# Clustered attention and a gated block: four more heads multiply with their centroids in 12 matmuls of 32 columns, in a re-ordered list of steps

## The chip, the cores and the metric

The kernel runs on one core of a Trainium2 chip. The core has five engines that run side by side, each with a queue of its own that it works through in order: TensorE (PE, matmuls; weight loads are shown apart as PEld), VectorE (DVE), ScalarE (ACT), GpSimd (POOL) and SyncE (SP), which here only issues DMAs. The metric is the device time of one execution in microseconds (us), lower is better.

## The reference

Four batches, eight heads, 768 tokens, 64 features per head. Each query and each key is assigned to the centroid, of 16 of its head, with the largest cosine. A query attends only to keys of its own centroid. A dense gated block follows.

```python
q_assign = np.argmax(np.einsum('bhsd,hcd->bhsc', q_n, c_n), axis=-1)
k_assign = np.argmax(np.einsum('bhsd,hcd->bhsc', k_n, c_n), axis=-1)
mask = q_assign[:, :, :, None] == k_assign[:, :, None, :]
scores = np.where(mask, scale * np.matmul(q, k.transpose(0, 1, 3, 2)), -1000000000.0)
scores = scores - np.max(scores, axis=-1, keepdims=True)
attn = np.exp(scores)
attn = attn / (np.sum(attn, axis=-1, keepdims=True) + 1e-09)
x = np.matmul(attn, v)                 # then (tokens, 512)
h = x @ w_in                           # 512 x 2048
out = (h * (1.0 / (1.0 + np.exp(-h)))) @ w_out   # 2048 x 512
```

Inputs and output are float32.

## The kernel before, in words

**Order.** The whole kernel after a short preamble is one list of some 1,550 words (`plan`, from line 722). A word is a step: `qk51` is step `qk` of number 51; after a point comes an engine (A = ACT, D = DVE, P = POOL) or the PSUM bank that it opens (0 to 3). The function `step` issues the word's instructions to their engines in the order of the list. So each engine meets its own instructions in list order, waits for what they read, and everything behind a waiting instruction on the same engine waits too. PE has four single banks and two double ones (`st`); a word that opens a bank waits until the last user of that bank has been read out.

**A head.** A head (b, h) has the number 8b + h. Its steps, in order:
- `r` loads queries and keys (two DMAs on SP); `vl` loads values (SP or POOL).
- `hi` and `lo` split the raw tile into two float16 parts (`lo` on DVE, L112; `hi` on ACT L103, POOL L105 or DVE L107).
- `ht` transposes it by a DMA on SP (L121) into the tile `ab`, for heads 8 to 31; heads 0 to 7 use PE and `ev`.
- `L` or `l` multiplies the 12 blocks of 128 tokens with the centroids on PE (L159). `L` does two matmuls of 16 columns for each block, which add up the two parts of the centroids in PSUM. `l` does one matmul of 32 columns, and `ls` (DVE, L168) then adds the two halves.
- `mx` (L183) and `ge` (L192), both on DVE, make the one-hot matrix of assignments.
- Heads 8 to 15: `cm` turns it on PE (L221), `ce` evicts it (ACT L232 or DVE L234) and sends it by a DMA on SP (L235) into spare rows of `ab`. Heads 16 to 31: `cs` scales on POOL (L199, L200), `cx` transposes by a DMA on SP (L208), `cv` moves it by a DMA on POOL (L212) into those rows. The rows make the mask part of the score matmul.
- `qk` (PE, L325, two matmuls of 384 columns, 192 of them) makes scores; `ex` (ACT, L330) the exponentials. Six `qk` belong to each head, three for each half of the queries. Heads 8 to 15 start at qk48, 51, 54 and so on; head 16 at qk96; head 21 at qk111; head 30 at qk162.
- `v` casts the values, `pv` (PE, L342) multiplies for two heads, `nm` (DVE, L352 and L354) normalizes, `pt` and `pe` or `xd` (a DMA on SP, L381) transpose the result.

**The dense block.** `e` (PE, L390, four matmuls) computes 128 of the 2048 hidden features for 384 tokens, `t` (ACT, L402) a tanh, `g` (DVE, L405) the gate. `w` loads weights by POOL; `wc` (DVE, L443) combines pieces of w_out once. For the second matrix one 128-token tile uses 16 plain matmuls in four words `b` (L417), with `bo` for its output, and pairs of tiles use Strassen's seven products `m` (L477), with sums `S` (DVE, L490), `z` (ACT, L499) and outputs `o` (L505, L508).

The two forms of the centroid product differ by the argument `w` of one function (line 149), and by where the list calls `ls`:

```python
        for n in ns or range(2 * m):
            i = min(n, job.n - 1)
            for x in range(0, 2 * HC, w):
                nc.tensor.matmul(
                    L[:, n % 2, :, n // 2], ab[:, i, :], stk[:, job.groups[i // 3][0], x : x + w],
                    start=(x == 0), stop=(x + w == 2 * HC),
                )
```

Of the kernel before, what the change touches and what calls it, by code (L numbers as in the profile page):

```python
# [29 lines left out]
def kernel(  # L30
# [573 lines left out]
    def step(op, n, eng, banks):  # L604
# [145 lines left out]
        ex74 qk76 m4 S14 xd9 xd8 ex75 qk77 z12 v14.A pv11.1 o13 ex76 r21 ge16 vl19 r22 hi22.P qk78 xd10 ht19 m14 nm11  # L750
        ex77 ex78 qk79 o1 ge18 pt11.1 o12 ex79 pe11.A m12.0 vl18.P o2 m13 qk80 o11 qk81 o10 pv12.0 ex80 qk82 ex81
        e34.2 v21.A nm12 ex82 qk83 ex83 e35.0 t35 lo22 qk84 e33.3 cs16 cs18 hi21.P cs17 r23 lo21 g35 pv13.1 qk85 t34
        g34 nm13 t33 g33 e36.0 cx16 v18.A ex84 qk86 e32.2 ex85 ex86 l19.3 ht20 vl20 ls19 t32 g32 vl22 t36 g36 qk87
        ex87 cx17 ht22 hi23.D e37.1 qk88 t37 g37 mx19 xd12 ex88 cx18 e40.3 ht21 t40 lo23 cv16 g40 cv17 e39.0 qk89 ex89
        t39 e41.2 ht23 l20.1 qk90 ex90 ls20 mx20 g39 qk91 ge20 t41 ex91 g41 pv14.3 vl24.P e38.1 t38 g38 qk92 ex92 qk93
        nm14 e43.2 t43 ge19 g43 ex93 e42.0 qk94 ex94 e45.1 t42 t45 g45 S23 e46.2 qk95 ex95 t46 g42 cv18 g46 cs19 qk96
        ex96 e44.3 cs20 qk97 ex97 xd13 xd14 pv15.1 nm15 cx19 cx20 l21.0 ls21 xd15 mx21 ge21 cs21 t44 g44 qk98 ex98
        e47.2 t47 g47 qk99 r25 m21.0 qk100 ex99 qk101 l22.1 ls22 mx22 m22.2 l23.3 z20 ex100 ex101 qk102 o20 ex102 ge22
        S21 ls23 qk103 pv16.2 cv19 ex103 qk104 e48.3 qk105 ex104 ex105 mx23 S22 m26 cs22 v22.D z21 t48 ge23 qk106
# [5 lines left out]
        xd18 e61.1 ht25 r27 ex119 ex120 g59 e62.2 t61 g61 t62 g62 mx24 qk121 ex121 qk122 ex122 S33 pv19.3 nm19 t60
        e63.1 r29 qk123 qk124 g60 m31.2 ex123 t63 ex124 ge24 lo26 g63 vl27.P S31 qk125 ex125 l25.3 ls25 m32.0 qk126
        ex126 m37 qk127 qk128 ex127 z30 S32 pv20.3 m36 hi27.D o30 ex128 lo27 vl28 qk129 qk130 ht26 z31 m35 nm20 ex129
        ht27 lo28 z32 qk131 l26.1 m41.3 o33 m34 S43 ls26 mx26 xd19 ge26 S34 S41 cs26 S42 mx25 cs24 cx26 ex130 qk132
        vl29.P ex131 qk133 pv21.1 nm21 z40 l27.0 ex132 qk134 ex133 m33 S44 m47 ex134 ge25 qk135 qk136 ls27 m46 cx24
        ht28 cs25 cx25 cv26 cv25 ex135 z41 hi29.D o31 m42.1 r30 ex136 e65.0 m45 xd21 o32 t65 qk137 qk138 z42 g65 o43  # L770
        e64.2 ex137 ex138 m44 m43 o41 t64 e66.0 mx27 o40 qk139 cv24 lo29 ge27 t66 g66 qk140 ex139 ex140 o42 g64 cs27
        cx27 pv22.1 e67.3 qk141 nm22 e68.0 v25.A qk142 l28.1 t67 g67 hi30.D ls28 mx28 ex141 e70.3 ex142 vl31 t68 ge28
        e69.2 cs28 qk143 t70 qk144 e71.1 g70 e72.3 t69 g69 ex143 ex144 qk145 g68 r31 t71 xd20 g71 e73.2 t72 lo30 g72
        qk146 ex145 ex146 pv23.0 nm23 t73 g73 qk147 qk148 e74.3 ex147 t74 S53 g74 ex148 e75.1 t75 hi31.D e76.0 t76 g75
# [55 lines left out]
```

## Time and profile before

| | us |
|---|---|
| median of 3 runs (lowest, highest) | 300.97 (300.54, 301.33) |
| the profiled execution | 301.45 |
| its span, first to last instruction | 299.7 |
| PE busy | 289.5 |
| ACT busy | 233.6 |
| DVE busy | 222.1 |
| POOL busy | 72.6 |

All numbers from the profile are of one execution. "Busy" is the time in which an engine executes something; waiting and issuing a DMA do not count. A row of the kind `L159 PE ... x304 | 9.8, 176` is a group of instructions of one source line: the count, the busy time in us, the mean duration of one in ns, and then the idle time before them with what ended it. A row of the timeline starts with its start and its length in us; brackets hold the idle time of that engine just before. A row of the chain of waits has start, length and what the end of the kernel was waiting for in that time. A row of windows has the stretch, its length and the busy time of each engine. "DMA to landing" is the time from issue to the last byte.

### The profile page before, as it was taken

How to read it: one execution, taken by the hardware profiler on the slowest of the kernel's cores; microseconds unless marked ns; L12 is line 12 of the kernel's file. 1: busy time of each engine (PE TensorE's matmuls, PEld its weight loads, DVE VectorE, ACT ScalarE, POOL GpSimd, SP SyncE). 2: the span in 40 equal slices, each digit the busy share in tenths (PEclk: the TensorE clock that was granted, in tenths of full speed). 3: DMA queues.
4: the chain of work that ended last, by engine and by line, in shares of the span. 5: the costliest groups of instructions: out<-in, count | busy, mean ns of one | idle time of the engine just before them, and what ended most of it. 6: DMA issues, size and time to landing. Idle time of an engine off the chain costs nothing.

```text
span 299.7 us, 8579 instructions
## 1 busy us (share of the span) xinstructions
PE 289.5 (97%) x3433; PEld 212.7 (71%) x3433; DVE 222.1 (74%) x482; ACT 233.6 (78%) x410; POOL 72.6 (24%) x125
## 2 busy tenths in 40 slices
...
GB/s 209 293 252 240 195 195 174 188 239 217 232 201 160 171 180 266 182 166 103 133 212 202 166 68 112 248 158 125 52 88 35 26 5 79 74 28 35 38 18 126
DMA packets 75368, 44.13 MB, mean 147 GB/s; under 512 B 54288, under 2 KB 71216, under 8 KB 75328
## 3 DMA queue, kind: packets, MB, share of 16 engines
q1 hardware_dynamic: 70560, 36.14, 51.2%
...
HBM read 27.30 MB, written 6.29 MB: 112 GB/s over the span
## 4 chain that ended last, share of the span: by engine, by line
PE 74%; DMA 13%; ACT 4%; DVE 3%; issue 2%; SPq 1%; POOL 1%; ACTq 0%; DVEq 0%; POOLq 0%
PE ph L390 22%; PE xb L477 18%; PE pS L325 15%; PE pO L342 9%; DMA vn<-in_v_dram 6%; DMA ab<-hl 4%; PE yb L477 3%; PE psN L159 3%; ACT P L330 2%; PE po L417 2%; DMA ab<-cdt 1%; DMA ab<-cd 1%; DMA raw<-in_q_dram 1%; PE wb L477 1%; DVE hl L112 1%
## 5 line engine op out<-in xcount | busy, mean ns | idle before, releaser
L330 ACT ACTIVATE P<-pS 128x768 f16<-128x768 f32 x192 | 151.2, 816 | 21.6 <-PE pS L325 20.1
L390 PE MATMUL ph<-xt,win_s 128*128 128x384 f16 x512 | 96.4, 326 | 0.0
L405 DVE SCALAR_TENSOR_TENSOR gt<-tn,ph 128x384 f16<-128x384 f32 x128 | 68.0, 550 | 32.8 <-ACT tn L402 32.0
L325 PE MATMUL pS<-ab 128*128 128x384 f16 x384 | 87.1, 326 | 1.4 <-DMA ab<-cdt 0.8
L402 ACT ACTIVATE tn<-ph 128x384 f32<-128x384 f32 x128 | 60.8, 499 | 13.5 <-PE ph L390 10.2
L390 PEld LDWEIGHTS <-win_s 128*128 128x128 f16 x512 | 49.4, 98 | 30.8
L325 PEld LDWEIGHTS <-ab 128*128 128x128 f16 x384 | 34.3, 98 | 17.8 <-DMA ab<-cdt 1.1
L342 PEld LDWEIGHTS <-P 128*128 128x128 f16 x1152 | 39.8, 97 | 4.2 <-DVE cd L234 0.4
L342 PE MATMUL pO<-vt,P 128*128 128x65 f16 x1152 | 41.2, 193 | 0.0
L477 PEld LDWEIGHTS <-gt 128*128 128x128 f16 x352 | 33.9, 98 | 6.4 <-DVE xn L354 0.3
L112 DVE SCALAR_TENSOR_TENSOR hl<-raw,hl 128x768 f16<-128x768 f32 (+3 forms) x35 | 31.4, 901 | 0.6 <-ACT hl L103 0.3
L105 POOL TENSOR_SCALAR hl<-raw 128x768 f16<-128x768 f32 (+1 forms) x11 | 22.8, 2074 | 34.9 <-DMA raw<-in_k_dram 20.2
L477 PEld LDWEIGHTS <-s 128*128 128x128 f16 x264 | 25.5, 98 | 4.5
L159 PEld LDWEIGHTS <-ab 128*128 128x128 f16 x544 | 18.9, 97 | 6.3 <-DMA ab<-hl 2.1
L477 PE MATMUL xb<-wout_s,gt 128*128 128x256 f16 x176 | 22.7, 273 | 0.2 <-DVE xn L354 0.2
L499 ACT ACTIVATE ot<-xb 128x256 f32<-128x256 f32 x33 | 12.7, 386 | 12.3 <-PE xb L477 12.0
L159 PE MATMUL psN<-stk,ab 128*128 128x16 f16 (+1 forms) x544 | 20.1, 184 | 1.7 <-DMA ab<-hl 0.7
L477 PE MATMUL xb<-wc,s 128*128 128x256 f16 x160 | 20.7, 273 | 0.0
L354 DVE TENSOR_TENSOR xn<-pO,zr 128x384 f16<-128x384 f32 x32 | 17.8, 557 | 1.1
L199 POOL TENSOR_SCALAR od<-od 128x96 f16<-128x96 f16 x16 | 8.9, 559 | 39.3 <-DVE od L192 39.1
L212 POOL DMA_DIRECT2D ab<-cdt x16 | 8.8, 547 | 33.2 <-PE pS L325 11.9
L490 DVE TENSOR_TENSOR s<-gt 128x1024 f16<-128x1024 f16 x22 | 15.7, 715 | 1.3 <-PE xb L477 1.0
...
## 6 DMA issues: line engine op xcount, KB each, us to landing
...
```

Of the source, the lines that this page charges most:

```text
L105: nc.gpsimd.tensor_scalar(out=o, in0=i, scalar1=QS, scalar2=None, op0=ALU.mult)
L112: nc.vector.scalar_tensor_tensor(out=hl[:, s, 1, :], in0=raws[job.name][:, s, :], scalar=QS, in1=hl[:, s, 0, :], op0=ALU.mult, op1=ALU.sub ...
L159: nc.tensor.matmul(L[:, n % 2, :, n // 2], ab[:, i, :], stk[:, job.groups[i // 3][0], x : x + w], start=(x == 0), stop=(x + w == 2 * HC),)
L325: nc.tensor.matmul(pS[:, e, 0:HALF], abs_[kj.name][:, kn, :], rhs, start=True, stop=True)
L330: nc.scalar.activation(out=P, in_=pst.pop(u)[:, :, 0:HALF], func=AF.Exp, bias=0.0, scale=ESC)
L342: nc.tensor.matmul(o[:, (2 * t + h) * VW : (2 * t + h + 1) * VW], Ps[i + h, c, j // 2][:, j % 2, ts(t, 128)], vtb[(i + h) % 13][:, j, 0:VW ...
L354: nc.vector.tensor_tensor(out=xn, in0=ov[:, :, 0:D], in1=zr.unsqueeze(2).to_broadcast([128, 2 * NM, D]), op=ALU.mult)
L390: nc.tensor.matmul(ph[:, 0:HALF], win_s[:, r, ts(fb, 128)], xts[b, c][:, r, :], start=(r == 0), stop=(r == NR - 1))
L402: nc.scalar.activation(out=tn, in_=phs[b, c, fb][:, 0:HALF], func=AF.Tanh, bias=0.0, scale=0.5)
L405: nc.vector.scalar_tensor_tensor(out=gt[:, fb, NM * c : NM * c + NM, :].rearrange("p t n -> p (t n)"), in0=tns.pop((b, c, fb)), scalar=1.0 ...
L477: nc.tensor.matmul(o, self.lhs(l, f), self.rhs(r, f), start=(f == 0 and opens), stop=(f == HB - 1), skip_group_check=True)
L490: nc.vector.tensor_tensor(out=o, in0=a, in1=b_, op=op)
```

## The change

The functions stay as they are. Only the list is replaced, from its 59th word on. In the new one heads 8, 10, 11 and 14, which had `L`, have `l` and `ls`; all other steps are the same ones, in another order, some in another bank or on another engine: the list first differs by a swap of tr4 and xr1, a shift of ge7 and of qk14, and from qk34 on everywhere. `hi` goes to ACT for heads 13, 15, 19, 21, 22, 28, 29 and 30 and leaves it for 14; it goes from POOL to DVE for 16, 18 and 26 and from DVE to POOL for 24 and 27. `vl` goes to POOL for 14, 15, 17, 20 and 28 and to SP for 16, 18, 24, 25 and 27. `v` changes engine for 8, 10, 13, 15, 16, 18, 19, 20, 24, 25, 28 and 31; `ce` for 12, 13 and 15; `pe` for 11 and 31. The diff, cut to the stretches spoken of below:

```diff
@@ -722,76 +722,76 @@
...
-        w9 t1 e5.2 qk30 ex30 w11 g3 lo9 r13 vl8 qk31 t5 pv4.3 qk32 ex31 nm4 e8.1 g1 g5 qk33 lo10 e13.3 r12 ex32 qk34
-        ex33 ht8 ht10 t8 t13 e11.2 g13 g8 ex34 e14.0 t11 g11 hi11.D wc4 qk35 pt4.3 qk36 e2.1 e10.2 ex35 qk37 pe4.D
-        ex36 t2 g2 t14 t10 qk38 g10 g14 ex37 ht9 e15.3 t15 pv5.1 nm5 r14 qk39 e12.2 ex38 lo11 wc5 qk40 ex39 ex40 e7.1
-        t7 ht11 wc6 r15 qk41 e9.0 g15 t12 ex41 qk42 t9 b0.3 qk43 g7 b1 ex42 wc0 qk44 g12 g9 hi13.D L8.1 ex43 b2 qk45
-        lo13 mx8 L10.2 ge8 cm8 mx10 ex44 b3 ex45 ce8.A wc1 ge10 bo0 pv6.1 nm6 qk46 l9.0 cm10 vl15 ht13 ls9 mx9 wc2 ge9
-        qk47 hi12.A lo12 vl13 ht12 wc12 b4.3 ce10.A ex46 pt6.2 b5 cm9.0 ex47 hi14.A ce9.A pe6.A lo14 r16 pv7.1 nm7 b6
-        L11.2 wc8 pt5.0 pe5.A pt7.1 pe7.A b7 mx11 ge11 cm11 v10.A v8.A ce11.A hi15.D qk48 e24.0 r17 ht14 bo1 lo15 ht15
-        vl9 v11 vl14 vl16.P t24 g24 e21.3 t21 e18.2 qk49 g21 ex48 l13.1 ls13 mx13 e22.3 t18 g18 ex49 qk50 r18 l12.1
-        ls12 mx12 v15.D ex50 e27.0 t27 g27 vl17 hi17.P t22 g22 hi16.P e20.2 t20 g20 qk51 e19.1 ge12 e16.0 qk52 e23.3
-        ex51 qk53 t16 t19 g19 g16 ex52 t23 ex53 e29.2 t29 g23 cm12.1 ce12.D ge13 qk54 ex54 e26.0 g29 e30.3 t30 t26
-        e25.1 t25 qk55 ex55 qk56 v13.D l15.2 g30 g26 ls15 g25 e17.3 t17 e28.0 lo16 od2 qk57 cm13.1 e31.2 g17 S3 ex56
-        wc13 wc14 ce13.A qk58 r20 ht16 v9 pv8.3 nm8 ex57 qk59 ex58 qk60 t31 L14.1 ex59 ex60 m1.3 mx15 wc7 mx14 ge15
-        g31 qk61 qk62 ge14 t28 g28 m7 wc15 S13 ex61 ex62 lo17 cm14 ce14.A wc9 hi18.P lo18 cm15.0 ce15.A m11.2 wc3 qk63
-        qk64 v16 pv9.1 nm9 z0 v17 ht17 r19 S1 ex63 ex64 qk65 m2.0 vl21.P qk66 ex65 z10 S2 wc10 S4 S11 wc11 ex66 qk67
...
-        qk107 ex106 ex107 nm16 S24 r24 cx21 v20 m25 z22 m27.1 cx22 cv20 qk108 v19 pv17.2 qk109 o23 hi24.D vl23.P cs23
-        xd16 cx23 v23.D cv21 ex108 qk110 m23 cv22 ex109 g48 nm17 o21 m24 o22 ex110 qk111 lo24 ht24 e49.2 ex111 qk112
...
-        m56 ex154 cv28 qk156 ex155 g81 ls29 l30.3 mx29 ls30 ge29 cs29 mx30 ht31 qk157 t82 g82 ex156 cx29 ge30 cs30
-        vl30.P e80.0 z51 t80 qk158 m57 l31.3 ex157 v29 ex158 m52.2 o50 ls31 m55 z52 o53 g80 pv25.2 e85.3 nm25 e83.0
-        t83 t85 e89.2 mx31 g85 ge31 m54 m53 cv29 qk159 g83 cx30 o51 cv30 t89 ex159 cs31 e90.3 cx31 o52 g89 qk160 t90
-        g90 e87.0 qk161 e86.2 ex160 t87 g87 ex161 e84.3 t84 g84 v30.A t86 g86 S63 qk162 e88.0 v28 pv26.1 t88 ex162 g88
...
-        m91.3 m97 z90 m102.2 m101.1 m96 S103 m107.0 z100 z91 m95 S101 S94 z92 o100 S102 m106 z101 m93 o91 o93 S104
-        m105 z102 o103 m92.2 o90 m94 o92 m104 o102 m103 o101
...
+        w9 t1 e5.2 qk30 ex30 w11 g3 lo9 r13 vl8 qk31 t5 pv4.3 g1 qk32 ex31 nm4 e8.1 g5 qk33 lo10 e13.3 r12 ex32 qk34
+        ex33 ht8 ht10 t8 t13 qk35 ex34 ex35 hi11.D g13 g8 e11.2 e14.0 t11 qk36 v10 e7.3 pt4.1 qk37 ht9 lo11 ht11 ex36
+        g11 e9.2 t7 g7 t14 g14 qk38 ex37 t9 g9 e15.3 ex38 wc4 pe4.D wc0 wc1 t15 qk39 ex39 g15 wc2 wc5 e10.0 qk40 pv5.2
+        nm5 wc8 ex40 t10 g10 qk41 ex41 e12.3 qk42 e2.1 pv6.2 t2 g2 qk43 b0.0 t12 g12 nm6 l8.1 ls8 ex42 qk44 ex43 qk45
+        mx8 r15 hi13.A lo13 ge8 ht13 pt6.2 l10.1 ls10 ex44 mx10 pt5.3 ge10 wc6 b1 b2 l9.1 pe6.A ex45 r14 hi12.A qk46
+        ls9 mx9 ge9 qk47 pe5.A ex46 ex47 b3 cm8.3 ce8.A b4.1 lo12 hi15.A b5 v11 ht12 r16 bo0 wc12 l11.2 ls11 mx11
+        pv7.3 nm7 lo15 ht15 cm9.0 ge11 ce9.A cm10.2 b6 pt7.3 b7 wc13 bo1 hi14.D ce10.A pe7.A e27.3 t27 g27 e24.0 e22.1
+        e18.2 t24 t22 g24 g22 l13.0 e23.3 qk48 t18 ls13 t23 r17 g18 mx13 vl9 lo14 cm11.0 ht14 l12.1 ls12 hi16.D g23
+        e25.2 qk49 ex48 qk50 ce11.A ex49 t25 ex50 g25 e21.0 lo16 ht16 t21 g21 e30.1 t30 g30 qk51 e28.3 ex51 e20.2 t20
+        ge13 g20 qk52 v8 e19.0 t28 g28 t19 g19 mx12 ge12 od1 ex52 e16.1 t16 e26.2 t26 g26 g16 qk53 ex53 e29.0 t29
+        hi17.P qk54 r18 l14.3 ls14 qk55 vl13 r19 ex54 g29 cm12.2 ce12.A e31.1 qk56 ex55 t31 wc9 cm13.3 mx14 ce13.D
+        l15.2 ls15 g31 mx15 wc10 e17.0 qk57 ex56 ex57 ge14 ge15 m1.3 qk58 qk59 t17 ex58 g17 r20 wc3 hi18.D v9 pv8.1
+        od2 vl16 ex59 wc14 cm15.2 ce15.D S3 lo18 cm14.0 ce14.A qk60 ex60 qk61 S1 lo17 S2 nm8 m2.0 z0 o0 qk62 pv9.2 S4
+        nm9 v13 ex61 ex62 qk63 wc7 ex63 qk64 ex64 vl17.P m7 vl14.P qk65 m6 hi20.D l16.1 qk66 ex65 qk67 wc15 hi19.A
...
+        nm16 ex105 cs21 cx21 S24 m26 z21 t49 hi24.P g49 cv20 cs22 cx22 cv21 qk106 e50.3 ex106 ge23 qk107 ex107 m25
+        vl23.P t50 z22 v18.D r25 lo24 g50 v24.A qk108 e51.2 e53.1 ex108 t51 m23 vl22 g51 r28 qk109 qk110 pv17.3 v20.A
+        cs23 cx23 ex109 qk111 o21 nm17 m27.2 ex110 ex111 o23 cv22 ht24 e52.3 t52 qk112 cv23 g52 qk113 hi25.P v23.D t53
...
+        e81.1 nm24 t81 e82.0 t82 g82 m56 z51 ht30 g81 cv27 qk153 qk154 ex153 ex154 m55 ht31 l30.1 l31.0 ls30 m57 z52
+        qk155 cv28 e80.2 qk156 ls31 v31 e87.1 mx30 t80 ex155 g80 ge30 cs29 cx29 cv29 m52.0 o50 t87 S54 g87 o53 cs30
+        qk157 e85.2 ex156 e89.0 t85 qk158 mx31 ge31 cx30 cv30 cs31 cx31 g85 ex157 ex158 t89 e83.1 t83 g89 qk159 g83
+        ex159 m53 o51 qk160 xd24 e91.2 t91 pv25.1 nm25 qk161 ex160 m54 g91 o52 qk162 ex161 e86.2 e84.0 qk163 ex162
+        e88.3 t84 g84 t86 t88 g88 qk164 pv26.1 e90.0 ex163 ex164 g86 nm26 S63 t90 g90 e94.2 e93.3 t93 g93 t94 g94 cv31
...
+        g124 t126 g126 e125.1 t125 g125 m101.3 m91.2 m97.0 m102.1 S91 S92 S103 z90 m96 z100 o100 m107.1 S94 z91 m95
+        z92 S101 S102 m106 o93 z101 m93 S104 o91 m105 z102 o103 m94 o92 m103 o101 m104 m92.2 o102 o90
```

More of the change, by code (lines that the diff above doesn't have):

```diff
@@ L750 @@
[L750 to L759, printed above, removed]
@@ L760 @@
-        qk107 ex106 ex107 nm16 S24 r24 cx21 v20 m25 z22 m27.1 cx22 cv20 qk108 v19 pv17.2 qk109 o23 hi24.D vl23.P cs23
-        xd16 cx23 v23.D cv21 ex108 qk110 m23 cv22 ex109 g48 nm17 o21 m24 o22 ex110 qk111 lo24 ht24 e49.2 ex111 qk112
-        e50.1 cv23 t49 vl25.P ex112 g49 qk113 xd17 e51.3 v24 t50 ex113 qk114 g50 e52.2 t51 pv18.0 ex114 g51 t52 e53.1
-        nm18 qk115 t53 g52 ex115 e54.3 g53 vl26.P hi25.P v26 t54 g54 e55.2 r26 t55 g55 qk116 ex116 e57.1 e56.3 lo25
-        r28 qk117 qk118 t56 g56 e58.2 l24.0 ls24 ex117 ex118 qk119 e59.3 t57 g57 qk120 e60.0 t58 g58 t59 hi26.P hi28.D
@@ L765 @@
[L765 to L774, printed above, removed]
@@ new lines @@
+        xd8 v14.A v17 xd10 ls18 mx18 ge18 l17.0 ex74 qk76 vl19 xd9 r21 pv11.1 ht20 ex75 qk77 ex76 z11 ls17 o3 qk78
+        nm11 m4 cs18 pt11.1 m15 ex77 ex78 hi22.A z12 o2 qk79 pe11.D S14 ex79 r23 qk80 pv12.0 lo22 ht22 qk81 ex80 ex81
+        hi21.A o13 nm12 ht19 e34.1 t34 g34 m13 qk82 ex82 qk83 ex83 lo21 ht21 e35.0 t35 hi23.D cs16 o1 g35 qk84 m14
+        e33.1 qk85 cx16 cx18 mx17 ge17 t33 g33 lo23 ht23 o12 cs17 cx17 ex84 o11 ex85 pv13.3 e36.1 t36 qk86 e32.0 g36
+        l19.2 qk87 e39.1 ex86 qk88 ls19 nm13 t32 g32 l20.2 ls20 ex87 ex88 e40.3 mx19 ge19 t40 qk89 qk90 vl20.P e38.2
@@ new lines @@
+        ex89 mx20 t39 t38 g40 xd12 g39 e37.0 t37 qk91 cs19 cv16 g37 pv14.3 cx19 ge20 ex90 ex91 cv17 qk92 ex92 l21.0
+        e43.1 nm14 qk93 r24 xd13 vl18 xd14 e41.3 vl24 ex93 ls21 g38 S23 t43 qk94 ex94 g43 e46.0 t41 g41 qk95 ex95
+        v21.A e44.2 t44 mx21 e45.1 qk96 qk97 cs20 v19.D ge21 g44 cv18 pv15.3 e42.2 ex96 qk98 nm15 xd15 t45 g45 ex97
+        qk99 t46 t42 g46 l23.3 ls23 e47.1 cv19 g42 ex98 m21.0 qk100 t47 cx20 g47 S21 ex99 ex100 l22.3 qk101 ex101 z20
+        ls22 m22.2 o20 mx22 ge22 qk102 ex102 r26 e48.3 t48 qk103 mx23 g48 pv16.1 e49.2 qk104 ex103 qk105 ex104 S22
@@ new lines @@
+        nm16 ex105 cs21 cx21 S24 m26 z21 t49 hi24.P g49 cv20 cs22 cx22 cv21 qk106 e50.3 ex106 ge23 qk107 ex107 m25
+        vl23.P t50 z22 v18.D r25 lo24 g50 v24.A qk108 e51.2 e53.1 ex108 t51 m23 vl22 g51 r28 qk109 qk110 pv17.3 v20.A
+        cs23 cx23 ex109 qk111 o21 nm17 m27.2 ex110 ex111 o23 cv22 ht24 e52.3 t52 qk112 cv23 g52 qk113 hi25.P v23.D t53
+        g53 ex112 ex113 m24 o22 e55.0 t55 vl26.P g55 lo25 qk114 v26 ht25 ex114 e56.3 t56 g56 vl25 r27 pv18.1 qk115
+        e54.2 nm18 ex115 hi26.D qk116 t54 g54 ex116 e58.0 vl27 t58 g58 lo26 r30 S33 qk117 ex117 e57.1 qk118 ex118 t57
@@ new lines @@
+        g57 e59.2 qk119 l24.3 qk120 e62.0 t59 g59 e60.1 m31.2 ex119 t62 g62 ex120 t60 hi28.A z30 v22.D ls24 g60 e61.0
+        e63.3 mx24 t63 qk121 qk122 t61 g63 ex121 ex122 m37 g61 S31 S32 m32.1 o30 qk123 ex123 qk124 l25.3 ht26 xd16
+        ge24 pv19.0 qk125 ex124 ex125 m36 lo28 ht28 nm19 l26.1 ls25 xd19 qk126 qk127 z31 m35 S34 ex126 m41.0 S43 ls26
+        ex127 qk128 ex128 m47 xd17 z32 hi27.P lo27 S41 S42 mx25 o33 hi30.A ge25 r31 ht27 pv20.1 nm20 qk129 qk130 m42.3
+        cs25 ex129 z40 m34 ex130 qk131 qk132 m33 o40 ex131 qk133 mx26 m46 cs24 xd18 ex132 ex133 cx24 r29 S44 lo30 ge26
@@ new lines @@
+        cv24 l28.3 o32 ls28 qk134 o31 qk135 z41 m45 ex134 ex135 qk136 ex136 mx28 pv21.2 nm21 qk137 qk138 z42 m43
+        hi31.D ex137 qk139 ex138 l27.3 o43 ls27 ex139 e64.1 t64 g64 hi29.A e66.2 qk140 e65.3 t65 xd20 cx25 m44 cv25
+        lo29 g65 ge28 t66 ex140 e70.1 t70 g66 g70 qk141 ex141 qk142 e69.3 t69 cs26 ht29 cs28 cx28 ex142 pv22.2 g69
+        qk143 cx26 nm22 mx27 ge27 o41 e71.3 ex143 t71 qk144 o42 e68.2 e67.1 t67 g71 g67 qk145 e73.3 pv23.0 ex144 qk146
+        t73 t68 g68 e72.1 e78.2 ex145 ex146 g73 nm23 v27.D e74.3 t72 t78 qk147 t74 g72 e76.0 ex147 t76 g78 g74 lo31
```

41 lines of the change are left out of this document (20 added, 21 removed).

## The prediction

> **What bounds the kernel now.** I read the page first, then the chain of waits in order of time, then the PE rows at each place where that chain leaves PE. On the page PE is busy for 97% of the span, and no other engine is above 78%.
>
> ```profile
> span 299.7 us, 8579 instructions
> ...
> PE 289.5 (97%) x3433; PEld 212.7 (71%) x3433; DVE 222.1 (74%) x482; ACT 233.6 (78%) x410; POOL 72.6 (24%) x125
> ```
>
> The profiled execution took 301.45 us: the span of 299.7 and 1.75 around it. It is 0.48 above the median of the runs, 300.97. The sum below is made on 301.45, and the last step moves it to the median.
>
> The chain lies on PE from 92 us to the end, with one hole. The pieces that matter, with the price of each kind of PE step among them:
>
> ```profile
> 49.25 10.96 DMA ab<-hl
> ...
> 63.81 1.10 PE pO L342 x36
> ...
> 72.24 1.31 PE ph L390 x8
> ...
> 73.93 3.94 DMA ab<-cd
> ...
> 92.68 0.87 PE xb L477 x8
> ...
> 101.41 0.65 PE pS L325 x4
> ...
> 146.69 4.00 DMA ab<-cdt
> ```
>
> So one `e` costs PE 0.65 us (1.31 for two), one `m` 0.87, one `pv` 1.10, one `qk` 0.33. I add these up between two words of a list and call the sum a distance. PE's own waits after 38 us, with the idle time in brackets (the last row is the weight load of the step at 85.24, which names the true releaser, a transpose):
>
> ```profile
> 60.25 0.77 PE L159 MATMUL psN<-stk,ab 128*128 128x16 f16 x24 [0.75 <-DMA ab<-hl]
> ...
> 77.92 0.50 PE L325 MATMUL pS<-ab 128*128 128x384 f16 x2 [0.37 <-DMA ab<-cd]
> ...
> 85.24 0.52 PE L159 MATMUL psN<-stk,ab 128*128 128x32 f16 x12 [0.54 <-DVE gt L405]
> ...
> 90.98 0.39 PE L477 MATMUL xb<-wout_s,gt 128*128 128x256 f16 x2 [0.17 <-DVE xn L354]
> ...
> 150.73 0.50 PE L325 MATMUL pS<-ab 128*128 128x384 f16 x2 [0.81 <-DMA ab<-cdt]
> ...
> 85.24 0.41 PEld L159 LDWEIGHTS <-ab 128*128 128x128 f16 x12 [0.93 <-DMA ab<-hl]
> ```
>
> The page models a matmul's end late: two `pS` matmuls show 0.50 us, but four take 0.65 in the chain and so follow each other at 0.16. The lost time is therefore the bracket plus about 0.16: 0.91, 0.53, 0.70, 0.32 and 0.97, together 3.4 us. This is all that a better order can win after 38 us, since the two lists hardly differ before their 35th qk.
>
> **The short form.** L8, L10, L11 and L14 (24 matmuls of 16 columns) become l8, l10, l11 and l14 (12 of 32). Start to start, with the step behind each:
>
> ```profile
> 65.07 0.51 PE L159 MATMUL psN<-stk,ab 128*128 128x32 f16 x12
> 65.42 0.29 PE L221 MATMUL psN<-ident,om 128*96 128x128 f16 x2
> ...
> 69.84 0.76 PE L159 MATMUL psN<-stk,ab 128*128 128x16 f16 x24
> 70.44 0.49 PE L363 MATMUL px<-ident,xn 128*128 128x128 f16 x6
> ```
>
> The long form takes 0.60 us, the short one 0.35: 0.25 saved, four times, **-1.0 us**, all on the path because PE is. The Trainium skill, "TensorE: Matmul & The Clock Gate", section "Wait — 56ns, not 53.3ns?", says that matmuls never start closer than about 25 ns however few columns they have. The trace agrees for 16 columns (0.60/24 = 25 ns) and not quite for 32 (0.35/12 = 29 ns); by the rule alone 48 matmuls fewer would save 1.2 us, and the time would come out 0.2 lower.
>
> What it adds on DVE, and the rows of the other steps that move (the last is two gates in a row):
>
> ```profile
> L168 DVE TENSOR_REDUCE L<-psN 128x192 f32<-128x384 f32 x20 | 11.1, 554 | 4.1 <-PE psN L159 4.0
> ...
> L183 DVE TENSOR_REDUCE mxn<-L 128x12 f32<-128x192 f32 x20 | 9.9, 497 | 0.3
> ...
> L183 DVE TENSOR_REDUCE mxn<-psN 128x12 f32<-128x192 f32 x6 | 2.1, 355 | 1.0 <-PE psN L159 1.0
> ...
> L107 DVE TENSOR_SCALAR hl<-raw 128x768 f16<-128x768 f32 x15 | 9.8, 654 | 1.7 <-DMA ab<-hl 1.7
> ...
> L405 DVE SCALAR_TENSOR_TENSOR gt<-tn,ph 128x384 f16<-128x384 f32 x128 | 68.0, 550 | 32.8 <-ACT tn L402 32.0
> ...
> L192 DVE TENSOR_TENSOR om<-L,mxn 128x192 f16<-128x192 f32 x4 | 1.4, 348 | 0.0
> ...
> L352 DVE RECIPROCAL zr<-pO 128x6 f32<-128x6 f32 x32 | 6.1, 191 | 8.7 <-PE pO L342 8.5
> ...
> L354 DVE TENSOR_TENSOR xn<-pO,zr 128x384 f16<-128x384 f32 x32 | 17.8, 557 | 1.1
> ...
> L272 DVE CAST vt<-vn 128x384 f16<-128x384 f32 x8 | 3.9, 483 | 0.8 <-DMA vn<-in_v_dram 0.8
> ...
> L490 DVE TENSOR_TENSOR s<-gt 128x1024 f16<-128x1024 f16 x22 | 15.7, 715 | 1.3 <-PE xb L477 1.0
> ...
> L103 ACT ACTIVATE hl<-raw 128x768 f16<-128x768 f32 x3 | 2.5, 842 | 0.0
> ...
> 57.54 1.01 DVE L405 SCALAR_TENSOR_TENSOR gt<-tn,ph 128x384 f16<-128x384 f32 x2
> ```
>
> Each head pays one `ls` (0.55) and a slower `mx` (0.50 for 0.36): 0.70, 2.8 us in all, and its one-hot matrix comes 0.70 later. I cost this at nothing on the path: in the new list the next PE step of the head, `cm`, stands 5.3 us (head 8) or more behind `l`. Without that cover the four heads would cost 2.8.
>
> **The reordering.** No step other than the four `ls` is added, so the time comes from waits. Each of the five, in the new list:
> - 60.25: PE waits for head 8's transpose. On SP the order r13 vl8 r12 ht8 ht10 ht9 is the same in both lists and l8 stands 0.1 us earlier. The wait stays: 1.0.
> - 77.92: qk51 waits for `ce9`, queued on SP behind ht12 and ce10. Now it is behind ht12, r16, bo0 and ht15 but ahead of ce10. From its place to qk51 there are 9.0 us, 9.6 before. Bounds: gone, or 0.5 as now. I take 0.2.
> - 85.24: l15 waits for its transpose, which stood behind r16, r17 and ht14 on SP. ht15 now stands ahead of r17 and ht14, 16 us of PE work ahead of l15. Gone. Late next is ht14, with 8.2 us to l14. The transpose at 49.25 took 11.0, but beside weight loads that are over by then, so the bounds are 0 and 2.8 and I take 0.
> - 90.98: m1 needs the bank that `nm8` frees, and nm8 was behind S3, wc13 and wc14 on DVE. In the new list m1 opens a bank that `ce13.D` frees. This is replaced by the DVE load below.
> - 150.73: qk111 waits for `cv21`. In the old list cv21 stands 2.1 us (qk110 m23 m24) ahead of it; in the new one qk106 e50 qk107 m25 qk108 e51 e53 m23 qk109 qk110 pv17 lie between: 6.4. A `cv` takes 2.0 to 4.0 to land. Gone.
>
> What covers the moved steps: SP keeps its number of DMAs (five `vl` go to POOL, five come back), and ACT gets seven `hi` more (0.84 each) less two `v` and one `ce`, some 4.4 us on 66 idle. POOL gives up three `hi` net. An ACT `hi` now holds the exps behind it until its raw tile has landed; the nearest is hi15, 5.3 us behind r15, and behind it stand ce9, ce10, pe7 and ex48, so its price lies in the 0.2 of ce9. The new place that I see is DVE between l8 and pv8:
>
> ```profile
> 60.25:88.30 28.05, 27.14 (x329) 17.95 (x330) 24.39 (x51) 20.57 (x40) 5.79 (x6) 1.00 1.00 233
> ```
>
> The columns are length, PE, PEld, DVE, ACT, POOL. DVE is busy for 24.4 of 28.05 us. Between the same two steps the new list has 4 `ls`, 2 `mx`, 2 `ge`, 2 `hi` and 2 `g` more, and one `nm`, two `v` and one S fewer. By the rows above that is 6.3 - 2.4 = 3.9: DVE would work 28.3, or some 0.6 less, since steps in a row overlap (two gates take 1.01, not 1.10), against 27.7 of PE work by distances. The cover is gone there. Bounds: nothing, if the overlap comes and DVE loses its 3.7 of idle time (28.05 - 24.39), and 28.3 + 3.7 - 27.7 = 4.3 if neither happens. An engine that falls behind loses its idle time first, and steps that PE needs only later (wc9, wc10, wc3, hi18) stand in this stretch and may slip, so I take 0.8, near the lower end.
>
> Head 30 is tighter too: from ge30 to qk162 it is 7.9 us, 12.3 before, for cs, cx and cv (0.56 + 0.38, 2.3 to 5.6, 2.0 to 4.0 by these rows):
>
> ```profile
> L199 POOL TENSOR_SCALAR od<-od 128x96 f16<-128x96 f16 x16 | 8.9, 559 | 39.3 <-DVE od L192 39.1
> ...
> L200 POOL TENSOR_SCALAR od<-od 128x96 f16<-128x96 f16 x16 | 6.1, 383 | 0.0
> ...
> L208 SPq DMA_TRANSPOSE cdt<-od x16: 1167/1182/2243, 116.1 to 221.4; - x16
> ...
> DMA to landing us min/median/max: 2.3/3.2/5.6
> ...
> L212 POOL DMA_DIRECT2D ab<-cdt x16: 522/542/588, 122.0 to 224.4; - x16
> ...
> DMA to landing us min/median/max: 2.0/2.9/4.0
> ```
>
> Between 5.2 and 10.5 for 7.9: 0 to 2.6 lost; medians make 7.0, so I take 0.3 for this and its like.
>
> A new wait comes ahead of l8: `wc8` stands 17 words ahead of l8, at about 55 us, and needs the last piece of wout_s, issued at 46.39 with 6.9 to 11.1 to land (`L529`), so 53.3 to 57.5. Behind it are g10, g2, and with them b0. wc8, g10 and g2 make 1.4 and b0 0.86, so l8 could start at 59.8 at worst, inside its wait until 60.25: nothing. Without ht8's wait it would cost about 0.6.
>
> ```profile
> 46.39 0.75 POOL L529 DMA_DIRECT2D wout_s<-in_moe_w_out_dram  x1 [0.53 <-issue]
> ...
> DMA to landing us min/median/max: 6.9/9.4/11.1
> ```
>
> **The sum.** -1.0 for the short form; -3.4 for the old waits; +1.0, +0.2, +0.8 and +0.3 for the new ones: -2.1. 301.45 - 2.1 = 299.35 for an execution like the profiled one, and 298.9 against the median.
>
> **The rivals.**
> - Only l8's wait is left. The DVE stretch and head 30 cost nothing: -1.0 - 3.4 + 1.0 = -3.4, so 297.5. For it: the old list runs 92 to 146 and 151 to the end without a hole. Against: the DVE load.
> - The waits move and keep their sum, as SP is still one queue with 11 us transposes in it: -1.0 alone, 300.0.
> - Slower: DVE becomes the bound from l8 to pv8. Nothing overlaps, the idle time stays, because DVE waits for `t` and `psN` in order and each late gate holds a PE bank, and the stretch costs its upper bound: -1.0 - 3.4 + 1.0 + 0.2 + 0.3 + 4.3 = +1.4, so 302.4. For it: 24.4 of 28.05 already. Against: wc, hi and lo wait for nothing of PE's, so a DVE that is behind always has work. It decides from 3.8 us upwards, where the sum passes +0.9.
>
> **How the numbers follow.** A measurement of this kernel can tell about 0.3% (0.9 us) from no change. Forecast 42% (297.7 to 300.0), only l8 left 15%, waits that move 21%, DVE the bound 22%. Faster by over 0.3% (below 300.07) are the first two and a quarter of the third: 0.62. Same: most of the third: 0.17. Slower: 0.21. The range 297.3 to 301.9 leaves out the ends of the first rival and of the last; the forecast's own is 297.7 to 300.0.
>
> **What would show it.** l8 to l11 and l14 as 12 matmuls of 0.35 us, and 24 `L168` reductions for 20. PE waits at l8 until about 60.2, and nowhere for `cdt` at qk111. DVE near full from 60 to 90 us with no PE bracket over 0.5 there. The forecast is wrong if DVE releases PE for more than 2 us in that stretch, if `cx30` or `cv30` is what qk162 waits for, or if ht10 or ce9 land later than in the old trace.

## The result, and the profile after

The changed kernel takes 301.91 us (median of 20 runs, 299.93 to 303.66), the kernel before 300.30 beside it (20 runs, 298.35 to 302.07): ratio 1.0054, interval 1.0034 to 1.0074. A second measurement gave 1.0046 (1.0024 to 1.0068). It is slower by about half a per cent, some 1.5 us; 298.9 us and "faster" were forecast.

The profiled execution took 300.97 us, which is less than the profiled 301.45 of before, though the medians stand the other way round: the one trace was drawn 0.9 us below its median, the other 1.15 above. The page and the groups of lines of the changed kernel:

```profile
span 298.8 us, 8491 instructions
...
PE 289.0 (97%) x3385; PEld 211.8 (71%) x3385; DVE 221.5 (74%) x484; ACT 235.7 (79%) x414; POOL 67.3 (23%) x123
...
L168 DVE TENSOR_REDUCE L<-psN 128x192 f32<-128x384 f32 x24 | 13.2, 553 | 3.5 <-PE psN L159 3.5
```

The same groups kept apart by shape show the 48 matmuls of 32 columns more (288, 240 before) and the 96 of 16 fewer (208, 304 before):

```profile
L159 PE MATMUL psN<-stk,ab 128*128 128x32 f16 x288 | 12.2, 193 | 0.2 <-DMA ab<-hl 0.2
L159 PE MATMUL psN<-stk,ab 128*128 128x16 f16 x208 | 6.8, 176 | 0.4 <-DVE xt L374 0.4
```

In the chain of waits, head 10's transpose, there behind the weight load of wout_s, has taken the place of head 8's (49.25, 10.96), and the pieces of `cd` at 73.93 and `cdt` at 146.69 are gone. New in it are pieces of DVE and ACT:

```profile
47.17 7.83 DMA wout_s<-in_moe_w_out_dram
55.00 7.07 DMA ab<-hl
...
121.25 0.57 DVE gt L405
...
181.68 0.39 ACT ot L499
...
288.43 0.70 DVE s L490
```

PE is still busy for 97%, and DVE has the 24 reductions. The time has to be looked for in PE's waits. As in the prediction, I add 0.16 to a bracket behind a `pS` matmul. PE rows of the timeline of the changed kernel (start, length, then in brackets the idle time before and its releaser):

```profile
52.34 0.81 PE L390 MATMUL ph<-xt,win_s 128*128 128x384 f16 x4 [0.27 <-DVE gt L405]
...
62.11 0.52 PE L159 MATMUL psN<-stk,ab 128*128 128x32 f16 x12 [0.19 <-DMA ab<-hl]
...
120.88 0.48 PE L325 MATMUL pS<-ab 128*128 128x384 f16 x2 [0.17 <-ACT P L330]
121.86 0.81 PE L390 MATMUL ph<-xt,win_s 128*128 128x384 f16 x4 [0.49 <-DVE gt L405]
...
182.11 1.03 PE L477 MATMUL xb<-wout_s,gt 128*128 128x256 f16 x8 [0.74 <-ACT ot L499]
...
289.18 1.05 PE L477 MATMUL xb<-wc,s 128*128 128x256 f16 x8 [0.30 <-DVE s L490]
```

None of the five waits of the profiled execution of before is left. Others stand in their place: 0.43 at e9, 0.35 at l10 (head 10's transpose), 0.33 and 0.65 at qk87 and e39, 0.90 at m45, 0.47 at m106. All but l10's stand at four places (qk87 and e39 are neighbours), 2.8 us with two small ones at 47.8 and 115.3 left out, and appear nowhere in the prediction. Their releasers are gates, an exponential, a snapshot and a sum, not DMAs.

### The profile page after: what moved, and what is told of

Read it like the earlier page. It is cut to its first block, busy times and chain, and to the rows that moved or that the text cites. A ratio compares the mean times of both kernels' runs of the same rounds, so it can differ in the third digit from the quotient of the medians.

```text
span 298.8 us, 8491 instructions
## 1 busy us (share of the span) xinstructions
PE 289.0 (97%) x3385; PEld 211.8 (71%) x3385; DVE 221.5 (74%) x484; ACT 235.7 (79%) x414; POOL 67.3 (23%) x123
## 4 chain that ended last, share of the span: by engine, by line
PE 76%; DMA 13%; ACT 4%; DVE 3%; issue 2%; SPq 0%; POOL 0%; ACTq 0%; DVEq 0%; POOLq 0%
PE ph L390 25%; PE xb L477 16%; PE pS L325 16%; PE pO L342 9%; DMA vn<-in_v_dram 5%; DMA ab<-hl 4%; PE psN L159 3%; PE yb L477 3%; DMA wout_s<-in_moe_w_out_dram 3%; PE po L417 2%; ACT P L330 2%; PE wb L477 1%; DMA raw<-in_q_dram 1%; DVE hl L112 1%; ACT hl L103 1%
## 5 line engine op out<-in xcount | busy, mean ns | idle before, releaser
L402 ACT ACTIVATE tn<-ph 128x384 f32<-128x384 f32 x128 | 61.7, 505 | 16.3 <-PE ph L390 15.4
L325 PEld LDWEIGHTS <-ab 128*128 128x128 f16 x384 | 34.3, 98 | 16.8 <-issue 1.3
L105 POOL TENSOR_SCALAR hl<-raw 128x768 f16<-128x768 f32 (+1 forms) x8 | 16.5, 2066 | 33.9 <-DVE gt L405 28.6
L159 PEld LDWEIGHTS <-ab 128*128 128x128 f16 x496 | 17.9, 97 | 4.4 <-issue 0.6
L199 POOL TENSOR_SCALAR od<-od 128x96 f16<-128x96 f16 x16 | 8.1, 505 | 53.4 <-DVE od L192 53.3
L477 PE MATMUL xb<-wc,s 128*128 128x256 f16 x152 | 19.7, 273 | 0.3 <-DVE s L490 0.3
L159 PE MATMUL psN<-stk,ab 128*128 128x32 f16 (+1 forms) x496 | 18.9, 186 | 0.5 <-DVE xt L374 0.4
L490 DVE TENSOR_TENSOR s<-gt 128x1024 f16<-128x1024 f16 x22 | 15.1, 687 | 1.0 <-DVE gt L490 0.5
```

The source lines that it names most:

```text
L105: nc.gpsimd.tensor_scalar(out=o, in0=i, scalar1=QS, scalar2=None, op0=ALU.mult)
L159: nc.tensor.matmul(L[:, n % 2, :, n // 2], ab[:, i, :], stk[:, job.groups[i // 3][0], x : x + w], start=(x == 0), stop=(x + w == 2 * HC),)
L325: nc.tensor.matmul(pS[:, e, 0:HALF], abs_[kj.name][:, kn, :], rhs, start=True, stop=True)
L402: nc.scalar.activation(out=tn, in_=phs[b, c, fb][:, 0:HALF], func=AF.Tanh, bias=0.0, scale=0.5)
L477: nc.tensor.matmul(o, self.lhs(l, f), self.rhs(r, f), start=(f == 0 and opens), stop=(f == HB - 1), skip_group_check=True)
L490: nc.vector.tensor_tensor(out=o, in0=a, in1=b_, op=op)
```

## The experiments

**The changed kernel again.** No edit.

> The changed kernel once more, for a second trace of it. Theory P (the new order makes waits of its own that do not depend on how long a transfer takes): the PE waits at 52.3 (0.43 us), 120.9 and 121.9 (0.33 and 0.65), 182.1 (0.91) and 289.2 (0.47) come back with the same size within 0.1 us, 2.8 us in all; what differs from the first trace is where PE waits for a DMA (head 10, head 14, the start). Rival Q (all waits of PE are chance landings of DMAs): these five change as the others do. Ratio to before 1.003 to 1.007 in both.

Measured: 302.19 us, ratio 1.0046 (1.0024 to 1.0068). The profiled execution took 303.02. The same places in its timeline, and three in which PE waited for a DMA:

```profile
51.48 0.81 PE L390 MATMUL ph<-xt,win_s 128*128 128x384 f16 x4 [0.42 <-DVE gt L405]
...
61.65 0.52 PE L159 MATMUL psN<-stk,ab 128*128 128x32 f16 x12 [0.60 <-DMA ab<-hl]
...
84.20 0.52 PE L159 MATMUL psN<-stk,ab 128*128 128x32 f16 x12 [0.47 <-DMA ab<-hl]
...
91.63 0.82 PE L325 MATMUL pS<-ab 128*128 128x384 f16 x4 [1.20 <-DMA ab<-cd]
...
122.81 0.48 PE L325 MATMUL pS<-ab 128*128 128x384 f16 x2 [0.16 <-ACT P L330]
123.78 0.81 PE L390 MATMUL ph<-xt,win_s 128*128 128x384 f16 x4 [0.49 <-DVE gt L405]
...
184.12 1.03 PE L477 MATMUL xb<-wout_s,gt 128*128 128x256 f16 x8 [0.75 <-ACT ot L499]
...
291.21 1.05 PE L477 MATMUL xb<-wc,s 128*128 128x256 f16 x8 [0.32 <-DVE s L490]
```

The waits for engines come back within 0.02 us, but for e9's (0.58 for 0.43). What differs is DMA: head 10's transpose (0.76 for 0.35), head 14's (0.63 at 84.20 for none), and qk60, which waited 1.36 for the rows of head 12 that `ce12` sends. Theory P holds but for e9, which changed by more than the 0.1 it allowed: the new order has lasting waits of its own, and a second kind that comes and goes.

**The kernel before, twice more.** No edit.

> The kernel before, once more, for a second trace. Theory W (the five waits of the first trace, 3.4 us, were in good part chance landings, and a sum made from one trace counted them as lasting): two or three of the waits at head 8, qk51, head 15, m1 and qk111 are gone or under 0.3 us, others are longer, and the sum of PE's waits after 38 us lies between 1.5 and 3.5 us. Rival (they are what the order gives, the same in every execution): the same five, each within 0.2 us of 0.91, 0.53, 0.70, 0.32 and 0.97.

> A third trace of the kernel before, on the same question: by theory W the five waits differ again from the first two traces; by the rival they are the same.

Measured: 301.24 and 299.47 us, one execution each. All PE rows with a bracket over 0.2 us from 55 to 95 us, first of the second trace, then of the third:

```profile
60.56 0.77 PE L159 MATMUL psN<-stk,ab 128*128 128x16 f16 x24 [0.98 <-DMA ab<-hl]
...
85.86 0.52 PE L159 MATMUL psN<-stk,ab 128*128 128x32 f16 x12 [1.39 <-DMA ab<-hl]
...
91.65 1.05 PE L477 MATMUL xb<-wout_s,gt 128*128 128x256 f16 x8 [0.22 <-DVE xn L354]
```

```profile
84.08 0.52 PE L159 MATMUL psN<-stk,ab 128*128 128x32 f16 x12 [1.25 <-DMA ab<-hl]
...
89.89 1.05 PE L477 MATMUL xb<-wout_s,gt 128*128 128x256 f16 x8 [0.24 <-DVE xn L354]
```

Of the five waits of the first trace, two last: l15 (0.70, 1.55, 1.41) and m1 (0.3 to 0.4). Head 8's transpose cost 0.91, 1.14 and nothing; qk51 and qk111 waited in the first trace alone. So the 3.4 us that the sum took away were made up of 1.0 at l15 and m1, which last, and 2.4 at head 8, qk51 and qk111, of which the two other traces show 1.1 and nothing. Theory W holds, in its make-up and in its sums: 3.4 in the second trace and 2.1 in the third, with 0.3 and 0.25 at cm15, where the rows have no bracket and the starts lie that much further apart.

**The short form in the old order.** The reductions stand right behind the products, and the one-hot products `cm` of these heads open a bank of their own; all else as before (diff cut):

```diff
-wc0 qk44 g12 g9 hi13.D L8.1 ex43 b2 qk45 lo13 mx8 L10.2 ge8 cm8 mx10
+wc0 qk44 g12 g9 hi13.D l8.1 ls8 ex43 b2 qk45 lo13 mx8 l10.2 ls10 ge8 cm8.1 mx10
...
-L11.2 wc8 pt5.0 pe5.A pt7.1 pe7.A b7 mx11 ge11 cm11
+l11.2 ls11 wc8 pt5.0 pe5.A pt7.1 pe7.A b7 mx11 ge11 cm11.2
...
-L14.1 ex59 ex60 m1.3
+l14.1 ls14 ex59 ex60 m1.3
```

> The order of before, and in it only the four heads in the short form (each with its reduction right behind it). Theory A (the short form is worth its PE time, and the new order gave it back): four times 0.25 us, 1.0 us faster than before, ratio about 0.9967. Rival B (the short form costs by itself, through 0.70 us more of DVE and a later one-hot matrix for each head): no gain or slower, ratio 1.000 to 1.005. In the trace A shows no new PE wait at the products that turn the one-hot matrices, B shows one of over 0.3 us at them or at the gates behind them.

Measured: 302.21 us, ratio 1.0063 (1.0037 to 1.0088): slower, as rival B has it and by more than its 1.005. The PE rows at the one-hot products of heads 8 and 11 and at m1:

```profile
63.03 0.31 PE L221 MATMUL psC<-ident,om 128*96 128x128 f16 x2 [0.91 <-DVE om L192]
...
72.53 0.31 PE L221 MATMUL psC<-ident,om 128*96 128x128 f16 x2 [0.58 <-DVE om L192]
...
91.26 1.05 PE L477 MATMUL xb<-wout_s,gt 128*128 128x256 f16 x8 [0.52 <-DVE xn L354]
```

The one-hot matrix (`om`) is late by the reduction: cm8 waits 1.07 us and cm11 0.74, and m1 0.68 where it waited 0.3 before. That is 2.2 us in three places, and the medians say 1.66 + 1.0 = 2.7 for what the reductions cost here. (The trace also has 0.98 at l24, where a transpose is late; it is not counted in.) So the short form does not pay in this order, which leaves it no distance. The new order has that distance, and neither trace of the changed kernel shows a PE wait for `om`.

**The new order without the short form's PE time.** The changed kernel, with the four products cut into twice as many matmuls:

```diff
+            if job.name in ("h8", "h10", "h11", "h14"):
+                for x in (0, HC):
+                    nc.tensor.matmul(
+                        L[:, n % 2, x : x + HC, n // 2], ab[:, i, :], stk[:, job.groups[i // 3][0], x : x + HC],
+                        start=True, stop=True,
+                    )
+                continue
```

> The order of the changed kernel, but the product of the four heads cut into 24 matmuls of 16 columns again (the reductions stay), so that only the PE time of the short form is taken back. Theory A: the order alone costs, so 1.0 us slower than the changed kernel, ratio to before 1.005 + 0.003 = about 1.009. Rival B (the short form is not on the path): ratio about 1.005, as the changed kernel.

Measured: 301.70 us, ratio 1.0044 (1.0023 to 1.0065), as the changed kernel or a shade faster. That is rival B's ratio; the 1.0 us of theory A did not show. The trace has the waits at e9, qk87, e39, m45 and m106 once more (0.57, 0.33, 0.65, 0.91 and 0.48), so they belong to the order and not to the products of 32 columns. In this trace head 10's transpose had landed when PE came to it, head 14's too, and qk60 did not wait. Whether the longer products cover these DMAs or the landings were lucky, one trace can't say.

**Half the new list, half the old.** Two joints at `pv12` (about 112 us): the first kernel is the new list as far as there and then what is left in the old order, the second the reverse, with the long forms. The words behind the joint (the first two lines are the changed kernel and the first joint, the last line is the second joint):

```diff
-pv12.0 lo22 ht22 qk81 ex80 ex81 hi21.A o13 nm12 ht19 e34.1
+pv12.0 mx17 ge17 o13 ht19 m14 o1 o12 vl18.P m13 o11 qk81 ex80 qk82 ex81 e34.2
...
+pv12.0 ht20 cs18 r23 lo22 ht22 ex80 ex81 hi21.A nm12 e34.1
```

> The new list up to pv12 (about 112 us), with the four short forms in it, and from there the order of before for all that is left. Theory A1 (the loss lies behind 112 us): faster than before, by the 1.0 us of the short form and up to 1.5 us of the old waits before 92 us: ratio 0.992 to 0.997. Rival A2 (the loss lies ahead of 112 us): slower, ratio 1.004 to 1.008.

> The other half: the list of before up to pv12, with the four long forms in it, and from there the order of the new list. Theory A1 (the loss lies behind 112 us): slower than before by 1.6 us and what the new head gains, ratio 1.005 to 1.013. Rival A2 (the loss lies ahead of 112 us): faster or the same, ratio 0.996 to 1.001, by the one old wait for cdt at qk111.

Measured: 301.70 us (1.0041, 1.0017 to 1.0064) and 308.94 us (1.0262, 1.0211 to 1.0313). Neither tells A1 from A2, because a joint makes waits that neither list has. The first has 1.7 us of them at 114.0 and 116.2 (an output on DVE and an exponential on ACT that are late). In the second PE stands for 5 us, and its clock is halved. PE row, then windows (stretch, its length, busy time of PE, PEld, DVE, ACT and POOL, the granted clock, DMA share, GB/s):

```profile
125.97 1.44 PE L390 MATMUL ph<-xt,win_s 128*128 128x384 f16 x4 [4.97 <-DVE gt L405]
```

```profile
118.00:121.00 3.00, 2.90 (x47) 2.04 (x45) 1.15 (x2) 2.86 (x6) 0.00 (x0) 1.00 1.08 189
121.00:126.00 5.00, 0.03 (x2) 0.02 (x1) 1.56 (x4) 0.51 (x1) 0.00 (x0) 0.74 1.23 202
126.00:129.30 3.30, 3.30 (x13) 1.58 (x13) 1.34 (x2) 1.30 (x2) 0.00 (x0) 0.50 0.50 105
129.30:133.00 3.70, 3.70 (x42) 2.51 (x40) 2.72 (x7) 2.60 (x5) 0.00 (x0) 0.87 0.68 130
```

The gate was late because `hi23.D` stood ahead of it on DVE and waited for its raw tile, whose second load SP issued only at 118.87 in this joint (5.49 us in the chain of waits).

**Four moves in the new list.** The four lasting waits, each undone where its releaser stood:

```diff
-ht9 lo11 ht11 ex36 g11 e9.2 t7 g7 t14 g14
+ht9 ex36 g11 e9.2 lo11 ht11 t7 g7 t14 g14
...
-lo23 ht23 o12 cs17 cx17 ex84 o11 ex85
+o12 cs17 cx17 ex84 o11 lo23 ht23 ex85
...
-r29 S44 lo30 ge26 cv24 l28.3 o32 ls28
+r29 lo30 ge26 cv24 l28.3 o32 S44 ls28
...
-m101.3 m91.2 m97.0 m102.1 S91 S92 S103 z90 m96 z100 o100 m107.1 S94 z91 m95 z92 S101 S102 m106
+S91 S92 m91.3 m97 z90 m102.2 m101.1 m96 S103 m107.0 z100 z91 m95 S101 S94 z92 o100 S102 m106
```

What the third edit goes for, in the trace of the changed kernel (DVE rows, then ACT rows):

```profile
179.21 0.69 DVE L490 TENSOR_TENSOR s<-gt,s 128x1024 f16<-128x1024 f16 x1 [1.50 <-PE xb L477]
179.81 0.95 DVE L112 SCALAR_TENSOR_TENSOR hl<-raw,hl 128x768 f16<-128x768 f32 x1
180.68 0.35 DVE L192 TENSOR_TENSOR od<-L,mxn 128x192 f16<-128x192 f32 x1
180.95 0.42 DVE L508 SCALAR_TENSOR_TENSOR ot<-xb,ot 128x256 f32<-128x256 f32 x1
...
181.40 0.38 ACT L505 ACTIVATE ot<-xb 128x256 f32<-128x256 f32 x1 [1.00 <-DVE ot L508]
181.68 0.38 ACT L499 ACTIVATE ot<-xb 128x256 f32<-128x256 f32 x1
```

S44 heads DVE's queue and waits 1.50 us for a product on PE; lo30, ge26 and o32 wait behind it although they could run; ACT's o31 waits for o32, the snapshot z41 comes after it, and m45 on PE needs z41. The place at 121.9 is of the same kind: lo23 (1.02 us) ahead of two outputs on DVE, so ACT stands for 1.2 us, the tanh t36 is late, its gate too, and e39 has no bank.

> The changed kernel with four moves of words and nothing else: g11 ahead of lo11 on VectorE (wait at 52.3); o12 and o11 ahead of lo23 (120.9 and 121.9); S44 behind lo30, ge26 and o32 (182.1); and the last words, from the first product of the last Strassen pair on, in the order of before (289.2). Theory P: the four places lose their 2.8 us of waits and nothing else changes, so 301.9 - 2.8 = 299.1, ratio to before 0.994 to 0.998, and no PE wait over 0.15 us is left at these places. Rival Q, or waits that only move on to the next place: ratio 1.002 to 1.007.

Measured: 300.25 us, ratio 0.9973 (0.9952 to 0.9995): 1.9 us faster than the changed kernel beside it, 2.8 expected. The PE rows:

```profile
53.03 0.81 PE L390 MATMUL ph<-xt,win_s 128*128 128x384 f16 x4 [0.20 <-DVE gt L405]
...
84.09 0.52 PE L159 MATMUL psN<-stk,ab 128*128 128x32 f16 x12 [0.52 <-DMA ab<-hl]
...
90.54 0.82 PE L325 MATMUL pS<-ab 128*128 128x384 f16 x4 [0.23 <-DMA ab<-cd]
...
121.92 0.81 PE L390 MATMUL ph<-xt,win_s 128*128 128x384 f16 x4
```

At 121.92 there is no bracket left, nor at m45 and m106. The wait at e9 went on to e15 (0.36), which needs g7, now behind lo11: that is 0.4 of the missing 0.9. The rest lies within what two medians of 12 runs can tell.

**Head 14's transpose sooner.** f4, and:

```diff
-e27.3 t27 g27 e24.0 e22.1 e18.2 t24 t22 g24 g22 l13.0 e23.3 qk48 t18 ls13 t23 r17 g18 mx13 vl9 lo14 cm11.0 ht14 l12.1
+e27.3 t27 g27 lo14 ht14 e24.0 e22.1 e18.2 t24 t22 g24 g22 l13.0 e23.3 qk48 t18 ls13 t23 r17 g18 mx13 vl9 cm11.0 l12.1
```

> f4, and lo14 with ht14 moved ahead, in front of e24 instead of behind l13, so that head 14's transpose is issued some 6 us sooner. Theory R (head 14's transpose, issued at 76.9 to 77.6 and landing 4.7 to 7.1 later, makes l14 at 83.1 to 83.9 wait for 0 to 1.4 us): a mean of 0.3 to 0.7 us faster than f4, ratio 0.992 to 0.997, and l14 never waits in the trace. Rival (the transpose was in time in nearly all executions, or the time returns at head 11 or 12): the same as f4 within 0.3 us.

Measured: 299.72 us, ratio 0.9963 (0.9933 to 0.9993), 0.5 below f4, which these intervals don't separate. l14 no longer waits. But l10 waits 1.40 for its transpose in this trace, and l13 0.71 for a gate that lo14 now holds up:

```profile
75.36 0.51 PE L159 MATMUL psN<-stk,ab 128*128 128x32 f16 x12 [0.55 <-DVE gt L405]
```

**The price of the short form, once more.** f5 with the four products cut as above.

> f5 with the product of heads 8, 10, 11 and 14 cut into 24 matmuls of 16 columns (the reductions stay): the price of the short form on TensorE alone, where fewer waits can swallow it. If the short form is worth its PE time on the path: 0.8 to 1.0 us slower than f5, ratio 0.003 higher. If DVE or a DMA sets the pace there and PE has the time: the same as f5 within 0.3 us.

Measured: 300.57 us, ratio 0.9983 (0.9959 to 1.0007), 0.85 above f5, as the PE time of the long products says. Against the pair on the unmended order (-0.2 us) this points the other way, and the intervals of both pairs overlap. In PE time the short form is worth 0.25 us for each head in every trace; how much of it reaches the end depends on whether PE then stands waiting for a transpose, and is not settled here.

**Four more places.** f5, with lo11 behind g14, lo14 behind g22, l10 behind b1, and cm12 with ce12 ahead of e29:

```diff
-e9.2 lo11 ht11 t7 g7 t14 g14
+e9.2 t7 g7 t14 g14 lo11 ht11
...
-g27 lo14 ht14 e24.0 e22.1 e18.2 t24 t22 g24 g22
+g27 e24.0 e22.1 e18.2 t24 t22 g24 g22 lo14 ht14
...
-pt6.2 l10.1 ls10 ex44 mx10 pt5.3 ge10 wc6 b1 b2 l9.1
+pt6.2 b1 l10.1 ls10 ex44 mx10 b2 pt5.3 ge10 wc6 l9.1
...
-qk53 ex53 e29.0
+qk53 cm12.3 ce12.A ex53 e29.0
```

> f5 with four more places mended: lo11 and ht11 also behind g7 and g14 (a wait of 0.36 us ahead of e15 in f4 and f5); lo14 and ht14 behind g22 and not ahead of e24, where they held up the gate that l13 waits for (0.71 us in f5); l10 behind b1 (0 to 1.4 us of waiting for head 10's transpose); cm12 and ce12 between qk53 and e29, some 3 us sooner, since ce12's transfer took 5.16 us to land and qk60 waited 1.37 for it in the second trace of the changed kernel. By theory P and R each place gives back what it cost: 1.0 to 2.0 us faster than f5, ratio to before 0.990 to 0.994. If the waits only move on: within 0.5 us of f5, ratio 0.995 to 0.998.

Measured: 299.51 us, ratio 0.9975 (0.9949 to 1.0002): the same as f5. Each wait I mended is gone and another has come:

```profile
56.55 0.81 PE L390 MATMUL ph<-xt,win_s 128*128 128x384 f16 x4 [0.36 <-DVE gt L405]
...
75.76 0.27 PE L221 MATMUL psC<-ident,om 128*96 128x128 f16 x2 [0.50 <-DVE L L168]
...
83.55 0.31 PE L221 MATMUL psC<-ident,om 128*96 128x128 f16 x2 [0.35 <-DVE om L192]
...
106.65 0.52 PE L159 MATMUL psN<-stk,ab 128*128 128x32 f16 x12 [0.33 <-DMA ab<-hl]
```

Three of the four are waits for DVE. The two at 75.76 and 83.55 lie in the stretch from l8 to pv8, where DVE is busy for 95% of the time in the changed kernel (26.70 of 27.99 us, windows below); that a step put first there makes another late fits this, but no run tests it alone. Here the waits do move on. f4 and f5 beat the kernel before, if only by 0.3 to 0.4%, and the changed kernel by more.

## Why the prediction was wrong

The step that failed is the sentence "No step other than the four `ls` is added, so the time comes from waits", followed by "Each of the five". It asked of the new list only whether the five old waits would be there, and at three more places (the stretch from l8 to pv8, qk162, and wc8 ahead of l8) what could come; waits anywhere else were put at nothing without a look. The new list has waits at e9, qk87 and e39, m45 and m106, 2.8 and 3.0 us in its two traces, and taking them out gave 1.9 us back. They could have been worked out: for m45, from S44's release (179.2) the queue is S44, lo30, ge26, o32 on DVE and o31, z41 on ACT, about 2.9 us by their rows, while PE has m46, l28, qk134 and qk135, 1.9 us, to fill.

The terms one by one:
- Short form, -1.0: right in PE time. That four heads without cover "would cost 2.8" stands too: in the old order they cost about 2.7, if the 1.0 of PE time was won there.
- Old waits, -3.4: right that all five go, wrong as a size. Three traces of before show 3.4, 3.4 and 2.1 in all, and the one summed came from an execution 1.15 us above the median. A sum made on it, and then moved to the median by 0.48 (the median of the 20 runs lies lower still), takes chance for gain.
- l8's wait, +1.0: did not come. ht8 landed 1.1 to 1.4 us ahead of l8 in both traces, 9.7 and 9.8 us behind its issue, where the trace that was summed had 10.96. qk51, +0.2: no wait, and qk162 waits for nothing, where 0.3 was put.
- The DVE stretch, +0.8, between 0 and 4.3: in the two traces it holds 0.35 and 1.56 us of waits, so the size was fair, but by luck: nearly all of it is l10 and l14 waiting for their transposes (0.35; 0.76 and 0.63), not DVE. DVE is nearly as full there as forecast, 26.7 and 27.2 us of work for 27.7 to 28.3. Windows of the first and of the second trace, from l8 to pv8:

```profile
60.59:88.58 27.99, 27.80 (x286) 18.06 (x285) 26.70 (x57) 22.54 (x43) 5.24 (x7) 1.00 1.04 224
```

```profile
59.73:88.93 29.20, 28.13 (x286) 17.96 (x285) 27.18 (x57) 22.75 (x43) 3.75 (x4) 1.00 0.98 210
```

- "Late next is ht14, with 8.2 us to l14 ... I take 0": mis-sized. By the list 8.2 us lie between them, but SP came to ht14 late: behind ce10's DMA, head 17's two loads and vl9. In the first trace its input lo14 was late on DVE as well, done at 77.13 for an issue at 77.38. SP's rows of the second trace:

```profile
75.44 0.57 SPq L235 DMA_DIRECT2D ab<-cd  x1
76.06 0.59 SPq L92 DMA_DIRECT2D raw<-in_q_dram  x1
76.71 0.42 SPq L92 DMA_DIRECT2D raw<-in_k_dram  x1
77.18 1.06 SPq L264 DMA_DIRECT2D vn<-in_v_dram  x1
78.34 1.32 SPq L121 DMA_TRANSPOSE ab<-hl  x1
```

It was issued 5.9 us ahead of l14 and landed 5.8 later. `ce12` at qk60 was not looked at; it cost nothing in the one trace and 1.36 in the other.

Put together: waits of 3.4 and 6.5 us in two traces after, 3.4, 3.4 and 2.1 before, so 2.0 more by the means, less 1.0 for the short form, is 1.0 slower, where 1.5 was measured. The 0.5 between is open; it is no more than the start of the kernel varies by chance (its 25th qk began at 36.6 to 37.0 us before and at 36.8 and 37.7 after, from nearly the same list).

In its mechanism the rival that the waits move came nearest, though they did not keep their sum. In time the slower rival did (302.4), but by luck, for it named the wrong cause: DVE did release PE, but behind waits of under 0.7 us each, and outside the stretch from l8 to pv8.
